# Spectra copied out of PSUM two banks at a time: a two-part layer on one core, with its stored order replaced

## The chip, the core and the metric

The program runs on one core of a Trainium2 chip. The time is device time in microseconds, the median of three runs. One core has five engines that run side by side: PE (TensorE, matmuls), DVE (VectorE), ACT (ScalarE), POOL (GpSimd) and SP, which here only issues DMAs. Matmul results land in PSUM, which has 8 banks of 512 fp32 columns per partition; ACT and DVE copy them from there to SBUF.

## The reference

Two independent halves are computed and put side by side in the output (2048 tokens, 640 + 640 columns). Part A is a gated long convolution, part B an attention with a compressive memory.

```
A: k_shift = 4-tap causal filter of k;  kv = k_shift * v
   y = irfft(rfft(kv, 2S) * rfft(ssm_k, 2S))[:S] + kv * ssm_D;   a = q * y
B: q, k, v = x @ wq, x @ wk, x @ wv          (32 heads of 20, segments of 512 tokens)
   for s in 4 segments:
       a_dot = softmax(q_s k_s^T * scale + mask) v_s
       a_mem = phi(q_s) M / (phi(q_s) z + 1e-6)
       o_s   = sigmoid(beta) * a_mem + (1 - sigmoid(beta)) * a_dot
       M, z += phi(k_s)^T v_s, sum phi(k_s)
   b = concat(o_s) @ wo
out = concat(a, b)                            (all inputs bf16)
```

## The kernel before

The whole program is recorded first and issued afterwards. `Layer` walks through the work and a `Recorder` notes each operation with its engine, its predecessors and its group of PSUM banks. `ORDER` is a stored permutation of the recorded operations, `BASE` gives each PSUM group its first bank, and `EVICT` has one digit per copy out of PSUM: "0" puts it on ACT, "1" on DVE. `Recorder.issue` then emits the operations in that order, so that on each engine, and on SP's queue of DMAs, the instructions stand exactly as the stored order has them. Every instruction carries line 257 in the profile, the line that issues it; the groups are told apart by the names of the tiles.

Part A runs in five passes `conv(dp)` of 128 channels. The filter (`kT`) and the filtered `kv` (`vt`) each go through `spectrum`: for each of 4 residues c, PE multiplies with the table `Wf` and makes two halves i = 0, 1 (real and imaginary part) of 512 columns, four matmuls of 256 columns each. They are copied to the tile `F`, which exists once. DVE then joins the residues in butterflies (`Xh` or `Kh`), multiplies the spectra (`product`, tiles `pq` and `Y`), and forms the inverse's inputs (`YB`, tile `Y`). `inverse` has for each c one PE group of 8 matmuls with `Wi` and one DVE multiplication with the loaded `q` (`pq<-ps,pq`), after which SP stores the rows. In the last pass each c is stored by itself, in 2 stores, 8 in all.

Part B has 8 units u, a segment and half of the heads each. `project(u)` makes `KQ` and `Va` (groups of five matmuls, 320 columns), turns `KQ` into `KQT`, and adds a row of bounds (`bT`, sent into `KQT` by small DMAs). `attend(u)` makes 10 score blocks of four banks; each is turned into the tile `ET` by two ACT exponentials of 1,024 columns. PE then multiplies `ET` with `Va` (and `PqT` with the memory `Mbd`), DVE divides. `project_out(s)` multiplies with `wo` and copies to `outb` (in the last segment: groups "ot" copied to `xT`, then five groups W copied to `PP`), and SP stores it. There are 80 score blocks and so 160 exponentials.

The copies of the spectra are made in this loop (lines 517 to 535); `FW` is the number of banks of a group:

```
for i in range(2):
    if i % FW == 0:
        g = self.group(FW, "F")
    ... four matmuls into g.ap[:, i % FW, :]
    if i % FW == FW - 1:
        self.evict(F[:, c, i - FW + 1:i + 1], g.ap, g)
```

Of the kernel before, what the change touches and what calls it, by code (L numbers as in the profile page):

```python
# [902 lines left out]
ORDER = r"""
c-jrtgMttW5Czb=Gk0=rwrjI(+um&3wry{=YqM?Jwr#$5zT(7@ToOeRNn%MN5hbZ4lPr>40wsl{lz1YNTk=SD$sqv}OQK3NNhPTztGFbTq?%14X>5rvd8M9E3J4^+#E_hlPx4D_O{Z}*nMRWOl3r738c8bw8eJ1=
PEDlgB)#O&1d>rQOAO7Txiqfi)~woCnoC2;qp7u^6p{>5TuMk&i7X|hl*E+6QbejsQK>G~q>+@CGNMve%1IN+Bqrshg5=eFT1;w4eyuE3q@q-kP!d<;X>!e=1vF4IYGO^Iku{2@(FPJE*|dc;liHG9(`rj;D>1dE
#L`+)P`gWeX(x51m2{O3Qb$@#AuX((rK5zFFp^1oYa0nGour3!llc-~i)sR0C`ELEjMgsFQ+i1s&8&TOj8@jD+D~t4RqZX|q>n6<eiBWqXkRI-#dU%%mvY))2FemyDigJome&-zNCru1T`Yqor54jNT1{(cbsZo>
WQY#cNjgXe>qs4?6||DBkd-o72kJ1Hq9wGX&d{M!QKxECt)oFYU7KlLt*14$zBbpHT1#u|8d)pDrGc)KS-M`f%MNL%vvs7j)AqVqw#Xa_*8Vy`8!4=bj*!OsPsgj+9POZ^WUl_y(egn*s@iuQp}%y4jFGVtBCU0t
Y?U_JR>#XUohzU8v;NR|I$uLsXj>)WWuB~-Vfsxb$pqOZV|Akp*KxW)Tj(Y^E(^7lMzUqPQzF_#31eYxvHp<d`dy~WE@`R1WQiV?JrZEMrK5Jz8M0SS$YJTKOSPN+mPOiGyXa5pu06D;9+M-oPd000+oHWRf=!jP
vQ_uXG&w2f<g}cZ5d9;kB#NDp12S2nn%gFwBGGN59+V3*Q)bB_S*?mS8p8}<^sru(n6_5G>QN=k9P6~69nnj2MZW1@`Kudrz1FwOLi;R&-?~Eo$!v*b!SY8}>Qz~#U9F9^wP@DOfY^3T4(Jy-s1YQN9nxL8TlZ*O
yCK_jyYA4PdQ6Y&UfrkB5d+tyxt-7mXkqazz9q8677?ATi|yBhc1F+YO*yCS?3Ub?a2DR~NEjrrrdAavwY}Yyut;J_EfktrWPFuyxG$$PH15fBIjxZpfbcl47xbcD(kQsBSM;j(vIlZaJ6K0cZPzuerLjlyLK@f&  # L910
ZD<drku|mymda9EZ)<6-?6EwP))p1f@Kl~icS~l;?WMezR}yGFETi?Y*OJ*{;*BInCTn7SEsLG7SjcLD$Y$9shvl?5NQ@*HXX7m?ZfP>4v-I{sGT2*rC$aI+`dMi!V`VKa(jm7!vg*iVc`cvCLwY>cCz{LhTYpP|
lt_itC}0UO&<0r|q(NGgv+`CA4>djt+FR>nkF=*%unc%+gYApGvl_^VAUwC>_SI^kgng8fcHf5BP#b3VG!yEgl#Q_ani&u5kBziKR>bb;T`g=`@Y`zRg}t<__$2jF2Su&8)k95uvj(`W-|fAPvJaLGf2|=Jp_o0;
7y42s*d%+Z*)h>x>l>|T9nlGuY=8;>Sq-afRV>JAS}kjhHpqdh)*iL3nt>hA60Pvrs++MXnqjg{u>`1N)%nI6u?ESUm}<YQHXE}s>aYpw+Gq>5TyQ?M3arRE_R+#}n$5KtHr;Zg2}7|dLo*D^@vW9;9^}PL`(*EQ
p3S#>m~9Jemc6oP`r5|Wb6sQMxX^ysI(uwmZIP|D#TK4FZKG|n&9>B**>YQ9`LV<*;fWQ1vN>9yE!Lwl+F`wgSY58PdfZ?e@Lmg|DywmoZMPj(1%*%;kr{!-P#mkRD0bOyi^3w<V|#6<ZLzIZ2K#KkMddb&#%An{
vgm?{JZOjPupP0Zwi(fRz=GJE$E+2*p%RZ<OIGF<)MR}&U~Kk9KMcex?TQd=L|hI+36w+(_D38Ba1+WQ5?eDCV{!o6vJHo$3b!I26R<pzFe&3R8M|W}dLTIiITXW?f+MgSdoUP7(2gD08-36VBQXjIxg9&O6T6U@
iI|<Ek&~rR8XcL1IXDj4I0l`VlG}NK7kQ6a`Is4*iY=I$wb+np_=MfqnPZWbnRuW3(S@0L0O@$0UD=&CI056)gSq&Wd6=Hhc$L?9jy;iqubG>tk(cLr29uDV1z3=USeQk4hwb@_MR}JetpY0Il=Wn9p0+p4$3eWp
Av|O6I1y*<oaOR9e9zk)%nNqW_F^B3F}L^U0A8{W{K&}|$WJWJ670oCEXgUjYzJ`&rC6F%F@mEwl4Upzec6vUIUTq7oG&<(!#RvcQQk{<Nq@=n_L*OJ3>7?w=k(DW!?B!!nYhHuoQ11amRD>Z=kqJSv7i_71-xb_
5scXw$5R;337p7DEat_1A*=c#KHx(x<{HdJexHN4oXiC{jCq)kg*bvGJdUX>;M2H_CoqN6IfF}C#b@%4-L<or#bD0iGAzduoX0uL<x+g-Z2qJ8T3ojq2ES#ut*n>xAH0BdSk9GP#noKHYJL%GxsEG%3D<E0Wqdtv
qlRC>9o)n%{Nz<!!v<c4x;Z_B8@Y*_`4D$;4_mmEk5JUN@iCs@H-r2S@8ba$;V;8@O|RuoQOd)4ZFev2ixJjW;2B;Zlt0HWuEa}(_BbBb^LTiV;1NBaNAkQL&l7oK-@%=%<4L@-NA+kP;L$yX*Y(IA#p`)}kLj-v
-}f_?-?M~%fU*4zZdw9Q>btm`2bs(ReHD`XA+AO$Z{V--77aaxr}i|S)>C>q&*163xwrIpXyJQU(JT30?qgg3fcBozGkIpu;!QlOzehXI?#=udvw2fL!lV3%R^G-7`*F_o)?UOvql0(!`M$tE;R_D4kyrQAJj1UT  # L920
=$(9?clN=4lBd|kyZSdY_Cemwhx-Wc?!Ej6dU#Lo?Z45-`}%i`^^qP*`}t4&MSuT;@jk$RVVsB7e;DFJ{r|>jI34C;bd)c2Xm}M}<Pmj(kM@a9o#c~!icj;^KHbOo44>(<e5x<@**?eD`*IKVrM|>B`3hg=D}9x(
@wL9e!)l1H^Nk)sUC;6aH~SXf=39N2Z}%O((|7wG-|PPY2lCQ8
"""
# [76 lines left out]
```

## Time and profile before

| what | value |
|---|---|
| median of 3 runs | 271.14 us (271.02 to 271.79) |
| profiled execution | 271.58 us, of it span 269.8 us |
| PE, DVE, ACT busy | 258.8, 249.6, 247.7 us |
| spectra copied on ACT | 71 of 512 columns, mean 682 ns of one |
| spectra copied on DVE | 9 of 512 columns, mean 683 ns of one |
| exponentials | 160 of 1,024 columns, mean 1,119 ns of one |
| granted TensorE clock | 1.00 |

The span goes from the first to the last instruction; the rest of the execution lies around it. Busy time counts an engine's instructions once where they overlap. The mean of one instruction includes its way through the engine's pipeline, which overlaps with the instruction behind it, so that the means of a full engine add up to more than its time. What one more instruction costs on a full engine is read from the starts of instructions that follow each other.

### The profile page before, as it was taken

What the parts mean: (1) busy time and instruction counts of PE and PEld (TensorE: products, weight loads), DVE (VectorE), ACT (ScalarE), POOL (GpSimd) and SP (SyncE); (2) the same over time, 40 slices, a digit from 0 to 9 for tenths busy, and PEclk for the clock granted to TensorE, in tenths of its full rate; (3) what the DMA queues carried; (4) which work ended last, traced back from release to release, by engine and by line L of the source; (5) the groups of instructions that cost most, each with busy time, mean ns of one, the idle gap of its engine ahead of it and who ended that gap; (6) DMA issues with size and microseconds to landing.
All of it is one profiled execution on the core that took longest, in us unless ns stands there. A gap on an engine that the chain in (4) does not pass through costs nothing.

```text
span 269.8 us, 10110 instructions
## 1 busy us (share of the span) xinstructions
PE 258.8 (96%) x4387; PEld 194.2 (72%) x4387; DVE 249.6 (93%) x400; ACT 247.7 (92%) x378; POOL 2.6 (1%) x9
## 2 busy tenths in 40 slices
PE   6999999999999999999999999999999999987994
PEld 3698677769777768767866778677776776655882
DVE  2899999999999999999999999999999999999960
ACT  1468899999999999999999999999999999999944
POOL 3000000000000000000000000000000000000000
PEclk9999999999999999999999999999999999999999
DMA  7998399995999799976999959987785289346043
GB/s 193 215 296 199 79 190 192 280 209 127 192 191 187 147 226 229 194 171 137 151 158 231 246 119 189 183 112 122 155 172 156 22 120 185 68 71 138 4 91 134
DMA packets 126716, 43.73 MB, mean 162 GB/s; under 512 B 117083, under 2 KB 124256, under 8 KB 126544
## 3 DMA queue, kind: packets, MB, share of 16 engines
q1 hardware_dynamic: 126512, 42.91, 80.7%
q8 instruction: 34, 0.56, 0.9%
q0 software_dynamic: 160, 0.19, 0.3%
q14 instruction: 10, 0.08, 0.1%
HBM read 14.11 MB, written 7.34 MB: 80 GB/s over the span
## 4 chain that ended last, share of the span: by engine, by line
PE 55%; ACT 35%; DMA 4%; issue 3%; DVE 1%; SPq 0%; ACTq 0%; DVEq 0%
PE ps L257 55%; ACT ET L257 23%; ACT F L257 5%; ACT PP L257 2%; ACT Va L257 2%; ACT KQ L257 2%; DMA out_dram<-outb 2%; DMA KQT<-KQ 1%; DMA pq<-in_A_q_dram 1%; ACT outb L257 1%; ACT xT L257 1%; ACT bT L257 0%; DVE xT L257 0%; DVE o_s L257 0%; DVE PP L257 0%
## 5 line engine op out<-in xcount | busy, mean ns | idle before, releaser
L257 ACT ACTIVATE ET<-ps 128x1024 bf16<-128x1024 f32 x160 | 163.6, 1119 | 1.1 <-PE ps L257 1.1
L257 PEld LDWEIGHTS <-xT 128*128 128x128 bf16 x640 | 58.1, 98 | 26.5 <-issue 4.8
L257 PE MATMUL ps<-wqkv,xT 128*128 128x320 bf16 x480 | 75.4, 299 | 0.4 <-DVE xT L257 0.2
L257 ACT CAST F<-ps 128x512 bf16<-128x512 f32 x71 | 41.9, 682 | 2.0 <-PE ps L257 2.0
L257 PE MATMUL ps<-Va,ET 128*128 128x21 bf16 x1280 | 40.1, 172 | 0.1
L257 PEld LDWEIGHTS <-ET 128*128 128x128 bf16 x1280 | 38.1, 96 | 1.9 <-issue 1.2
L257 PE MATMUL ps<-KQT 32*128 32x128 bf16 (+2 forms) x896 | 33.8, 238 | 0.8 <-ACT xT L257 0.4
L257 PEld LDWEIGHTS <-Wf 128*128 128x128 bf16 x320 | 29.2, 98 | 5.9 <-issue 1.7
L257 ACT CAST KQ<-ps 128x320 bf16<-128x320 f32 x55 | 25.8, 511 | 1.3 <-PE ps L257 1.1
L257 PE MATMUL ps<-wo,xT 128*128 128x320 bf16 (+4 forms) x160 | 25.7, 299 | 0.8 <-ACT ET L257 0.8
L257 PEld LDWEIGHTS <-KQT 32*128 32x128 bf16 x896 | 15.9, 91 | 11.7 <-issue 10.8
L257 PE MATMUL ps<-vt,Wf 128*128 128x256 bf16 x160 | 21.8, 272 | 0.1
L257 PE MATMUL ps<-kT,Wf 128*128 128x256 bf16 x160 | 21.8, 273 | 0.0
L257 PE MATMUL ps<-Y,Wi 128*128 128x256 bf16 x160 | 20.3, 273 | 0.6 <-ACT ET L257 0.3
L257 PE MATMUL ps<-Mbd,PqT 128*128 128x84 bf16 x96 | 18.1, 202 | 0.9 <-ACT ET L257 0.9
L257 DVE TENSOR_TENSOR Y<-Y,pq 128x2048 bf16<-128x2048 bf16 (+1 forms) x20 | 18.8, 946 | 0.1
L257 DVE TENSOR_TENSOR pq<-Xh,Kh 128x2048 bf16<-128x2048 bf16 x15 | 18.2, 1215 | 0.1
L257 PEld LDWEIGHTS <-Wi 128*128 128x128 bf16 x160 | 14.9, 98 | 4.2 <-issue 2.2
L257 ACT ACTIVATE PP<-KQ 128x1280 bf16<-128x1280 bf16 x12 | 16.4, 1368 | 0.0
L257 PEld LDWEIGHTS <-kr 128*128 128x128 bf16 x116 | 14.8, 148 | 1.7 <-issue 0.2
L257 ACT CAST Va<-ps 128x320 bf16<-128x320 f32 x29 | 14.7, 549 | 0.9 <-PE ps L257 0.9
L257 PE MATMUL ps<-pack 32*128 32x128 bf16 x512 | 13.8, 215 | 1.1 <-ACT ET L257 0.9
(90 smaller groups left out, 365.4 us busy)
## 6 DMA issues: line engine op xcount, KB each, us to landing
vt<-in_A_v_dram SPq DMA_DIRECT2D x10, 256.0 KB
pq<-in_A_q_dram SPq DMA_DIRECT2D x10, 256.0 KB
turned<-kT SPq DMA_DIRECT2D x4, 512.0 KB
kT<-turned SPq DMA_DIRECT2D x4, 512.0 KB
out_dram<-pq SPq DMA_DIRECT2D x8, 256.0 KB
out_dram<-outb SPq DMA_DIRECT2D x12, 160.0 KB
kb<-kr SPq DMA_DIRECT2D x6, 256.0 KB
Wf<-c_wf SPq DMA_DIRECT2D x4, 256.0 KB
```

The costliest lines, as they stand in the source:

```text
L257: f(*[fix(a) for a in args], **{k: fix(v) for k, v in kw.items()})
```

## The change

`FW` goes from 1 to 2. The two halves of a residue then share one group of two neighbouring banks, and one copy of 1,024 columns takes both after the second half's matmuls. There are 40 copies of spectra in place of 80, 38 on ACT and 2 on DVE. No matmul and no DMA is added or removed. Since the recorded operations are others, `ORDER`, `BASE` and `EVICT` are new as a whole: all engines and SP's queue have another order, and some other copies change between ACT and DVE.

```
--- before.py
+++ after.py
-EVICT = ("0101000110000010100000101000...
+EVICT = ("0000100010000001000000000000...
...
-KQW, FW, WW = 1, 1, 1
+KQW, FW, WW = 1, 2, 1
...
 ORDER = r"""
-c-jrtgMttW5Czb=Gk0=rwrjI(+um&3wry{=YqM?Jwr#$5zT(7@ToOeRNn%MN5hb...
+c-jrtgLW7S5Cy=ydw1KEscqY~o!Yi-+fHiRwr$(CZNK*ub0#lxAvPi+4iX{}vLg...
...
 BASE = r"""
-c-l>q0hYxe2m>Pu-v7p{L+ao9+FFH>1e?0o)Ht^kT4%O+7pwOjM5Oka@AEazxDo...
+c-l>q3lfAd2t$EVdjA_Qgn+B#*p}ZTqDoyZM@()$M_%qC*P6G(Qg%sO<XyYSwWP...
```

By kind, the copies of the two programs stand on the engines as follows; the copies of `PP` and `taps` are all on ACT in both.

| tile, columns | ACT before | DVE before | ACT now | DVE now |
|---|---|---|---|---|
| F, 512 | 71 | 9 | 0 | 0 |
| F, 1,024 | 0 | 0 | 38 | 2 |
| KQ, 320 | 55 | 9 | 52 | 12 |
| Va, 320 | 29 | 3 | 30 | 2 |
| bT, 512 | 8 | 0 | 7 | 1 |
| KQT, 512 | 7 | 1 | 7 | 1 |
| kT, 512 | 2 | 2 | 3 | 1 |
| xT, 512 | 4 | 1 | 5 | 0 |
| xT, 640 | 2 | 2 | 3 | 1 |
| outb, 320 | 19 | 5 | 19 | 5 |

The first place is ACT's list ahead of the first exponential (`ET`), from the copies that stand behind the filter's spectrum on, before:

```order
L257 CAST KQ<-ps 128x16x20 x3
L257 CAST KQT_87<-ps 128x4x128
L257 CAST KQ<-ps 128x16x20
L257 CAST KQT_87<-ps 128x4x128 x3
L257 CAST F_101<-ps 128x512 x3
L257 CAST bT_109<-ps 128x512
L257 CAST F_101<-ps 128x512 x3
L257 CAST Va_85<-ps 128x16x20
L257 CAST KQ<-ps 128x16x20
L257 CAST Va_85<-ps 128x16x20
L257 CAST KQ<-ps 128x16x20 x2
L257 ACTIVATE ET_114<-ps 128x1024
```

And now, with the filter's spectrum (the four wide copies):

```order
L257 CAST kT_100<-ps 128x4x128 x3
L257 CAST KQT_87<-ps 128x4x128 x4
L257 CAST F_101<-ps 128x1024 x4
L257 CAST KQT_87<-ps 128x4x128
L257 CAST bT_109<-ps 128x512
L257 CAST Va_85<-ps 128x16x20 x2
L257 CAST F_101<-ps 128x1024 x3
L257 CAST KQ<-ps 128x16x20 x2
L257 ACTIVATE ET_114<-ps 128x1024 x2
```

The 512-column copies have become wide ones, the first unit's copies of `KQ` and `KQT` that stood between the two spectra have moved ahead of them, and of the second unit's `KQ` two copies, not three, stand ahead of the first exponential; on PE as well one group of that projection has moved from ahead of the first score block to behind it.

The second place is the end of DVE's list, from the last butterflies of the fifth pass (`Y<-Xh`) on, before:

```order
L257 TENSOR_TENSOR Y_98<-Xh_104 128x2x512
L257 TENSOR_TENSOR pq_79<-ps,pq_79 128x4x128 x4
L257 CAST xT_97<-ps 128x512
L257 RECIPROCAL rr_118<-ps 128x32
L257 TENSOR_TENSOR o_s_110<-ps,rr_118 128x4x80 x2
L257 RECIPROCAL rr_119<-ps 128x32
L257 TENSOR_TENSOR o_s_110<-ps,rr_119 128x4x80 x2
```

And now:

```order
L257 TENSOR_TENSOR Y_98<-Xh_104 128x2x512 x2
L257 TENSOR_TENSOR pq_79<-ps,pq_79 128x4x128 x3
L257 RECIPROCAL rr_118<-ps 128x32
L257 TENSOR_TENSOR o_s_110<-ps,rr_118 128x4x80
L257 TENSOR_TENSOR pq_79<-ps,pq_79 128x4x128
L257 TENSOR_TENSOR o_s_110<-ps,rr_118 128x4x80
L257 RECIPROCAL rr_119<-ps 128x32
L257 TENSOR_TENSOR o_s_110<-ps,rr_119 128x4x80 x2
```

The fourth multiplication with `q` has moved behind the division of the last but one head group. On PE this goes with the inverse's groups: before, all four of the fifth pass stood ahead of the last score block (segment 3, second half, head group 3); now two of them stand behind it.

The third place is the start of SP's queue, before:

```order
L257 DMA Y_98<-in_B_x_dram 128x640 x2
L257 DMA ident<-c_ident 128x128
L257 DMA Y_98<-in_B_x_dram 128x640
L257 DMA wqkv<-in_B_wk_dram 128x5x320
L257 DMA Y_98<-in_B_x_dram 128x640
L257 DMA_TRANSPOSE kr<-in_A_k_dram 128x2048
L257 DMA Wf<-c_wf 128x1024
L257 DMA kT_99<-in_A_ssm_k_dram 128x2048
```

And now:

```order
L257 DMA Y_98<-in_B_x_dram 128x640 x4
L257 DMA ident<-c_ident 128x128
L257 DMA wqkv<-in_B_wk_dram 128x5x320
L257 DMA wqkv<-in_B_wq_dram 128x5x320
L257 DMA kT_99<-in_A_ssm_k_dram 128x2048
L257 DMA_TRANSPOSE kr<-in_A_k_dram 128x2048
L257 DMA Wf<-c_wf 128x1024 x3
```

All four loads of x now stand ahead of the identity, and the weights of q and the filter ahead of the transposing load of k.

More of the change, by code (lines that the diff above doesn't have):

```diff
@@ L897 @@
 TAP2 = (2, 3, 4)
-EVICT = ("0101000110000010100000101000000000000000000000000000000000000000001100000000001000000011010000100100000000000000000000000000000000000000"
-         "000010000100000000000100000000000000000000110000000010010010101001000100000000010000100100010000000")
-KQW, FW, WW = 1, 1, 1
+EVICT = ("0000100010000001000000000000000000000000000000100010000000011000100100000000000000000001100000000000000000000000000000010000000000000000"
+         "00000001010100000101000010000010000110000010111000000000000")
+KQW, FW, WW = 1, 2, 1
 KSW = (1, 1, 1, 1, 1)
@@ L903 @@
 ORDER = r"""
-c-jrtgMttW5Czb=Gk0=rwrjI(+um&3wry{=YqM?Jwr#$5zT(7@ToOeRNn%MN5hbZ4lPr>40wsl{lz1YNTk=SD$sqv}OQK3NNhPTztGFbTq?%14X>5rvd8M9E3J4^+#E_hlPx4D_O{Z}*nMRWOl3r738c8bw8eJ1=
-PEDlgB)#O&1d>rQOAO7Txiqfi)~woCnoC2;qp7u^6p{>5TuMk&i7X|hl*E+6QbejsQK>G~q>+@CGNMve%1IN+Bqrshg5=eFT1;w4eyuE3q@q-kP!d<;X>!e=1vF4IYGO^Iku{2@(FPJE*|dc;liHG9(`rj;D>1dE
-#L`+)P`gWeX(x51m2{O3Qb$@#AuX((rK5zFFp^1oYa0nGour3!llc-~i)sR0C`ELEjMgsFQ+i1s&8&TOj8@jD+D~t4RqZX|q>n6<eiBWqXkRI-#dU%%mvY))2FemyDigJome&-zNCru1T`Yqor54jNT1{(cbsZo>
@@ L907 @@
[L907 to L922, printed above, removed]
+c-jrtgLW7S5Cy=ydw1KEscqY~o!Yi-+fHiRwr$(CZNK*ub0#lxAvPi+4iX{}vLg%P0&pZo5+p@rBtr}&M+&4wDx^jZ<U|65LILDM8l*)n5Q+#e#6*77Mik^mJfuT<2=X94vLXXwAu8U>Pl*Q85As#A;i>!**RUE+
@@ new lines @@
+zX?<{Gom9CLTN@klZg6TiX*gsl;`qCiXyxQ>L*bxhJq-J7xGq0pb(1SyF}8+8b#~lois#L4MGI{A=H>!9u-g)Wl#={Q4!I!0V*L7kx&w)PzRM!8qqa|)<qM%me6=3jSx#?YdwTT6;wx61ZXvUme#0=F#1JWqA3E<
+49(F3VbBWg&;~Wo7VXgi9nl4y&>3CPP#bAwt)g)?wWif+h@;cdO4I0H`6sQlh0Z`cZK;Vgu{PEw+6_I?9aXiOCefGjN+u(zCe!&?fLhvIlWT2Fr|Gp9>S$e^iCIXY9W;Zc)C8JPXQK!5X)5iF{8~WgAfs;7teQ>Z
+Yj(|~nRN;pXcp~*9GX*$YkTdBTsjvew4KgFN$rP@+D7}MpcdAq+Dxl!O>L`%w37}*J*}@bbP1N?hAu;A9e|5^QwO1lUecm^UyJDpJ*f-vKo_Bl4#qPq$6|EV6<CSY7=o!-h4Xq>*WiM7(;nJg?`cmRfnJ(h`|B{|
+(NmgNPwO=uj_X=Zhhi-TXpolIC%O*LH5_(eCw5^yN@-~=qh)miD(EOw)RE||FVII{p|5VkR&2*cY{GNg(Q{f!cViFs;w7HyW<1mV*oOlcs}m877dlSI;|(U@r5?n19i?M*EXHAo7UyUks)td6qcH}<bhggXe)?M9
@@ new lines @@
+;{!fot`67N_=FMqMn~#fyu(8ssE_eT58*Se>K9zr!TMMWaF8CsExn=zd0XG=44tX(^cW`SB%Q2BF;PPhtRXrH@Aae3(^)!2r|JUzpeHb2b21mpuq=;bntswH`dPo?B&O>rY{6-q!C5TRrTPuuaYoN-Q5Iu(EY#ol
+gGKrSKe1e&V1?$DFZxwi>MC8V-}Nbe;V)L}8a<D-DkRtGdR6`dM5M56(2^|0e9X_kdJaGI0t)e;{!;L#7Umx<$K3p_LA;1px=AnL3N9lLv-2u)FrQTBZr!6sXIO?~cwR#UMr3)0Vg**^H@%J<$S*2|WC8CYG{bP4
+26DT)Q0^gs5ha2I%5B_1C7RsCErgcDOv1<vB~cia(O5ttF|34>Doo1gj3(6>RU%0YMwajrUAAa-)?_k9k*%77rKA>1%Y78#10-hxCSnY!&3)X@qb$v1%**YJ#e}TL9V{ZTC5+TzY@T5p)@MOE%et(`b8Nu4Y{>I`
+h*+|dF{OlT)<%4Uc&xzyY0O=W&t^Q%%Zwv&rKB`xOrBsdX~9<9p+)5Y53(hTOIax+<)k%JG8NnM3R5!;D@hy1m#eHOm1U>y(zJ{x>6n4nn4TG#iJ6&&UD%CHd7W9=g!^>A9?%=?%62@cx7eN?c$#VL2(#I3X18><
@@ new lines @@
+n+aqOJF*iyv#K28VOEi9a))=BP}18yCX$oPVE36=hVm4%F^LT0a88i!?7^Pw#nBwgz3k0P?8664CQ0Q2lgk*6;7C4X3cJXZ){p%;fR8wkgV>j&IFW-ni76$Rxn!?Sl$)H)DNG?#IgKIAYxyi##&JBeSTdWyAW3fJ
+We9UyTFGj;rGh->Oit%4&Solk$~nwqY2+n~+H20>T&A+rmQLpJ6{pA(=C{<6UY>EX<dF=LQ3}|5eq;{IXd#l*Cdmg@mrPdJYRMbE<8#)Ow|v2)dQ9s}4XGmyq>wd~#?nZdNNt%eGbEE_mQVb`*)pF+Y@&T;F)L_I
+rJ2l;7E(`IN-oPH&84`dv9D|;S>+o`+Dw@xrR)cP@;iU=HzU{|MzqqFP5v^_!dhzyXW?yyWtTD*+E!Xw+hzfl*<fO7hm;n^O4vUJSvf0j+bxo{5wi-m#iH15Yb$PBZN0UVg^X+)EUN9X=vG$_>oRLE9ps2cv%R*@
+mfInVVKFV1g|gVzNh(?#i)*!Ps!WsGwwO62r*xEfR>!K_T3aSHt%e=8<GNf{$U3WROSpnZY$@l;N>;ME)>-DsGS;*D7T*$BLQ7<ec+9#;Vw*2X?6|G5gSN_6+bTA&)!b#9t*bP&ZqmpW$O)@rNqsq!`9fJNi)4wc
@@ new lines @@
+;aFKJ-Q}c>lT+5%dP)yTY8$PYHMbVl)LPmmYhvB4hqbbJ9@7U&YwKyTyqBG}_}<&ravgg~A4}ltdB!%exAc*|wt)%#tVQ&5cHTC#p9OkyZ)07ozoqc5HbAy;EBi}ZYiI4PgY}h;cFnq3Rl8x=t&{Dy1J+LlN;Ml`
+E2Xmyv<nu=2ip)EYDev&ZR2>kWW#KgME2n}!fx6iyKN(7l&z7`cFRUd8Xse0ZMBTF%XZbqS#*!#>*R`!x52Ve()uRZEL&xW+_AeB%~Sh5TPs^+x9pN6p3Zm3Hi_%oWsgMhoif3qdP+~__w9jY@C}mDGkIpu<~wYs
+W%1$i&_38l+bgmCkv+C27HlIV#6H=6d1_fbj%W8Ap4)T!K6z%}?7RK21M<RV+H*T3LuHtZk@YgmKHFFOVh81=y|UN##{Sq_dvEXTh$QlVme~K=Py21~|I6jS{>QtUcXxC5P@c<+`E(mChoywiu;O083wme|@Gu_M
+3;9vW>$5GNhx70r!SnkuS!_$Juov-?UfNGcDL*b#?4+EQjht$eY_b*gnqJEn+9Eq8XC%Fs@v>gdgS@;~@Y<fo>w5#Q=ncJ+SN1Ai)z3;bZ|cpxhR?I=KF#La96KlHrJ2|9y57U<c`v^z7o@k(wM%kWdiq6a<c+<F
@@ L923 @@
+xA2zU$}h_mxhD7Ip*)h--p1ScO}Qm)y}ftvj^4>f_z>^oeZ8}H^)BAe$M{%(BK>`&UzZ#5SZ>Q5c_8;?l#ljtKHi7=03YbXe7Fzt!9Kw!da#H1Qd?kCe6mmSss0~tS+>s
 """
 BASE = r"""
-c-l>q0hYxe2m>Pu-v7p{L+ao9+FFH>1e?0o)Ht^kT4%O+7pwOjM5Oka@AEazxDoSwZQ?ptXT33&bJp3Po?V<|MMU1*1(wd<y%%fo&^Grv&xFYx34Riju$qsTK-rI1Qc=W?GfSg&ZK3(H3fE3}Pit?kt#%O6_!Blo
-?oV5xK`1J!3BCfccn91P_Xf-tJ831Yy3i`SkgyA@zxkhwWwyfqMo;^*(H3^SYbK-hrt3G~z_spPT2c39gV`Ml_>>v_ybvd$Bg%@~`NZk8`ed)`e4Un`3Dbd+q`KU@FrvVj_9yM0{^{O6AM$xDG)y=(`_GNxj&*PP
-3<Zw1r$y{$f7|V84&9aU7$-TyUmxG{A28mjSk7MlE98i>tMMGtKdv&T&$(&z?+pF{kIx1i
+c-l>q3lfAd2t$EVdjA_Qgn+B#*p}ZTqDoyZM@()$M_%qC*P6G(Qg%sO<XyYSwWP;^ef9yLI<w62a{qEwJ40+&Y5%flW(daBy5p*9AYK_S$SbtpTos|>OhFXnEv5^ahgiYsVF!Un@D@fG&YG&d?)IVBbv}c&{e~zu
@@ L928 @@
+UcojR39Gf93L0A-4Lm_TTG4~dO2+mYy`37$YIl}3(7&M0Fwb>Zt5z4P$?{D`Xa38+AE^5s(E5TsU{xyH*@L`74U8Pd{tY#QR$mSJ3py=59hbgC_)VPe1URb+X#0EhWI1Q8X&<v6X11kpcK2x-WSZ*z7YH)Wls<N<
+JK;0&@u%VU#SiB>P<tvW*?wyq1(^
 """
```

## The prediction

> **What bounds the kernel now.** I read the windows first, cut where the work changes its limit: from the start to the first score block on PE (32.28), from there to PE's first product with the last but one pair of exponentials (257.31), and the rest. The columns are the stretch, its length, then busy time and instructions of each engine.
>
> ```profile
> core 0: us, PE busy (x) PEld busy (x) DVE busy (x) ACT busy (x) POOL busy (x), PEclk, DMA share, GB/s
> 0.00:32.28 32.28, 29.87 (x258) 22.12 (x260) 24.53 (x48) 19.26 (x39) 2.57 (x9) 1.00 0.80 198
> 32.28:257.31 225.03, 220.08 (x3986) 165.43 (x3986) 221.90 (x346) 223.06 (x332) 0.00 (x0) 1.00 0.85 160
> 257.31:269.80 12.49, 8.82 (x147) 6.60 (x144) 3.18 (x7) 5.36 (x9) 0.00 (x0) 1.00 0.38 112
> ```
>
> In the first stretch PE is the fullest (29.87 of 32.28); ACT has little to do before there are scores. In the long middle ACT (223.06 of 225.03) and DVE (221.90) are both full, 99% each. PE's 220.08 is modelled, since matmuls overlap. In the last 12.5 us only PE is left, until its end at 266.14. The chain that ended last says the same of the end:
>
> ```profile
> 249.42 0.94 ACT ET L257
> 250.35 0.04 issue
> 250.40 15.75 PE ps L257 x300
> ```
>
> So a microsecond counts on PE before 32.28 and after some 250 to 257, and in between only if it is taken from ACT and DVE both. The waits then tell how much a smoother order could give back (engine and tile, whom it waited for, total, times, longest):
>
> ```profile
> ACT ET L257 <- PE ps L257: 1.1, 4, 0.4
> PE ps L257 <- ACT ET L257: 3.4, 10, 0.5
> ```
>
> No wait is long. What is lost lies in many small gaps, which the price list below makes visible.
>
> **What a copy costs.** Start, length, engine, instruction, count; a group's length holds the overlap of its members, so I take start to start.
>
> ```profile
> 61.62 1.40 ACT L257 ACTIVATE PP<-KQ 128x1280 bf16<-128x1280 bf16 x1
> 62.78 0.56 ACT L257 CAST KQ<-ps 128x320 bf16<-128x320 f32 x1
> 63.08 1.18 ACT L257 ACTIVATE ET<-ps 128x1024 bf16<-128x1024 f32 x1
> 64.00 1.72 ACT L257 CAST F<-ps 128x512 bf16<-128x512 f32 x3
> 65.42 1.47 ACT L257 ACTIVATE PP<-KQ 128x1280 bf16<-128x1280 bf16 x1
> 66.72 1.99 ACT L257 ACTIVATE ET<-ps 128x1024 bf16<-128x1024 f32 x2
> 68.55 1.63 ACT L257 CAST F<-ps 128x512 bf16<-128x512 f32 x3
> 69.96 2.06 ACT L257 ACTIVATE ET<-ps 128x1024 bf16<-128x1024 f32 x2
> ```
>
> Two exponentials take 68.55 - 66.72 = 1.83, so 0.915 each (0.92 at 63.08); three copies of 512 take 1.41 (and 1.42), so 0.47 each; a copy of 320 takes 0.30 to 0.31; an exponential of 1,280 takes 62.78 - 61.62 = 1.16. No ACT copy of 1,024 columns is in the trace. Its nearest row is ET, with the same columns, source and output: 0.91. The other end is two copies of 512, 0.94. A wide copy then saves 0.03 of a pair, between 0 and 0.05. 36 such pairs stood on ACT: about 1 us in all, not more.
>
> The Trainium skill, "ScalarE: Activation LUTs", section What ACT_TABLE_LOAD costs, gives an activation with immediate scale and bias as 186 ns + 0.833 ns a column, of which back-to-back ones overlap by about 93 ns. By that two copies of 512 would cost 1.04 us and a wide one 0.95, a saving of 0.09; the rows have 0.94 and 0.91, and so ACT's list would fall some 2 us further than in the sum below.
>
> **ACT's list in the middle.** Its rows for the stretch from 32.28 to 257.31 (busy time, mean of one, idle before):
>
> ```profile
> L257 ACT ACTIVATE ET<-ps 128x1024 bf16<-128x1024 f32 x159 | 162.7, 1120 | 1.1 <-PE ps L257 1.1
> L257 ACT CAST F<-ps 128x512 bf16<-128x512 f32 x59 | 35.4, 699 | 0.3 <-PE ps L257 0.2
> L257 ACT CAST KQ<-ps 128x320 bf16<-128x320 f32 x48 | 22.8, 523 | 0.1
> L257 ACT ACTIVATE PP<-KQ 128x1280 bf16<-128x1280 bf16 x11 | 15.1, 1376 | 0.0
> L257 ACT CAST Va<-ps 128x320 bf16<-128x320 f32 x27 | 13.8, 557 | 0.0
> L257 ACT CAST outb<-ps 128x320 bf16<-128x320 f32 x19 | 9.5, 502 | 0.5 <-DMA out_dram<-outb 0.5
> L257 ACT CAST bT<-ps 128x512 bf16<-128x512 f32 x7 | 4.6, 651 | 0.0
> ```
>
> 158 of the 159 exponentials count (the last belongs to the last score block), 47 of the KQ copies, and two copies of xT are not shown. At the prices: 158 x 0.91 = 143.8, 59 x 0.47 = 27.7, 93 copies of 320 x 0.31 = 28.8, 9 of 512 x 0.47 = 4.2, 11 x 1.16 = 12.8; sum 217.3. The stretch took 225.0, so 7.7 us were lost between ACT's instructions. In the new order the same stretch of ACT's list, counted, has 158 ET, 31 wide copies (28.2), 93 of 320, 6 bT and 1 xT (3.3), 11 PP: 216.9. That is 0.4 less (between 0.2 and 0.8, as the copy's price is rounded).
>
> **DVE's list in the middle.** From the first score block to the last butterfly of the fifth pass, on which PE's last inverse products wait:
>
> ```profile
> L257 DVE CAST F<-ps 128x512 bf16<-128x512 f32 x9 | 6.1, 683 | 0.1
> L257 DVE CAST KQ<-ps 128x320 bf16<-128x320 f32 x9 | 4.3, 485 | 0.6 <-ACT xT L257 0.6
> L257 DVE TENSOR_TENSOR o<-ps,rr 128x640 bf16<-128x640 f32 x16 | 13.0, 815 | 0.2
> L257 DVE TENSOR_TENSOR Xh<-Xh 128x1024 bf16<-128x1024 bf16 x20 | 13.6, 684 | 0.0
> 254.25 1.28 DVE L257 TENSOR_TENSOR pq<-ps,pq 128x512 bf16<-128x512 f32 x2
> ```
>
> From 320 to 640 columns out of PSUM the mean grows by 330 ns, so a wide DVE copy, which the trace does not have, is 815 + 384 x 1.03 = about 1.21 (bounds: 0.82 of the 640 columns and 1.37 of two copies). Five copies of 512 leave this stretch (-3.4), one wide one comes (+1.2), a KQ copy comes and a Va copy goes (0), one bT comes (+0.7), and three butterflies of 0.68 now stand ahead of the first score block (-2.1): -3.6. Six instructions fewer also means six overlaps fewer, 0.08 each (two multiplications of 0.685 take 1.28), so -3.1.
>
> **The end.** PE's inverse groups, and SP's stores:
>
> ```profile
> 252.23 1.91 PE L257 MATMUL ps<-Y,Wi 128*128 128x256 bf16 x16
> 254.07 0.41 PE L257 MATMUL ps<-pack 32*128 32x128 bf16 x16
> 254.63 1.92 PE L257 MATMUL ps<-Y,Wi 128*128 128x256 bf16 x16
> 254.97 6.70 SPq L257 DMA_DIRECT2D out_dram<-pq  x8
> 261.76 1.03 SPq L257 DMA_DIRECT2D out_dram<-outb  x2
> 264.88 2.23 SPq L257 DMA_DIRECT2D out_dram<-PP  x4
> 266.17 0.58 ACT L257 CAST PP<-ps 128x512 bf16<-128x512 f32 x1 [0.34 <-PE ps L257]
> ```
>
> Two groups take 254.07 - 252.23 = 1.8 us. Two of them now stand behind the last score block, so the path over ACT grows: 225.0 to 257.31, then 8.8 of PE to 266.14, becomes 225.0 - 0.4 and 8.8 + 1.8, which is +1.4 if every lost microsecond stays lost. The path over DVE was 222.1 (to 254.34) and 11.5 of PE from 254.63; it loses 3.1, and 1.6 of PE's rest, since only 9.9 follow the third inverse group (8.8 + 1.8 - 0.7 of products ahead of it): -4.7. Before, both ended together; now DVE has slack, and ACT alone is full.
>
> How much of ACT's 7.7 comes back with that? At least nothing. At most 5.0, if ACT then loses no more than DVE did (its busy 219.32 of the 222.06 to its last butterfly, 2.7):
>
> ```profile
> 32.28:254.34 222.06, 217.11 (x3942) 163.14 (x3945) 219.32 (x343) 220.73 (x329) 0.00 (x0) 1.00 0.86 161
> ```
>
> I take the middle, 2.6, since no row is nearer to either end. The first stretch has one projection group of five matmuls fewer ahead of the first score block:
>
> ```profile
> 30.82 1.52 PE L257 MATMUL ps<-wqkv,xT 128*128 128x320 bf16 x10
> 32.28 0.40 PE L257 MATMUL ps<-KQT 32*128 32x384 bf16 x8
> ```
>
> Ten take 1.46, five 0.7. But all four loads of x are queued ahead of the identity and more loads ahead of that of k, so I count half, -0.35 (between -0.7 and +0.7). The first of the eight stores waits for the third inverse group, 7.9 us ahead of PE's end, not 11.2 as now (254.97 against 266.14); with 6.7 for the eight and 1.0 for the two behind, the four last stores start 0.2 before PE's end, not 1.3. They need 2.0 to the last issue, which so comes 0.7 later; half of it counts, +0.35 (0 to +0.7).
>
> **The sum.** -0.4 + 1.8 - 2.6 - 0.35 + 0.35 = -1.2. The profiled execution took 271.58 (span 269.8), the median is 271.14; the change is taken off the median: 269.9. 0.3%, 0.8 us, is about what a measurement of this kernel can tell from no change.
>
> **Rivals.** *Nothing to measure.* ACT's list is as long as before, and a part of the lost time just covers the +1.4: 0.6 to 2.2 of the 7.7 return. For it speaks that ACT's waits in the rows are few; against it, that DVE, the other full engine, gets slack. Time 271.1.
>
> *The end gets longer, slower.* The two inverse products and eight stores behind the last score block cost 1.8, and nothing comes back, because ACT's gaps were its own and DVE's slack is useless. It decides once less than 0.6 of ACT's lost time returns. Time 272.5.
>
> *Banks.* A wide copy starts only after the second half's matmuls, 0.44 later (four of 0.11), and holds both banks until its end: 2 x (0.9 + 0.9) in place of 2 x (0.44 + 0.47), twice as long. If that doubles PE's 3.4 us of waits for ET's copies, and ACT starves for as long, 273.3 stands. Against it: 40 x 1.8 us are 4% of eight banks over the middle. The Trainium skill, "Perfetto Trace Analysis", section Matmuls, wants independent matmul groups to rotate through banks, so that the evacuation of one overlaps the next group's matmuls. That rule speaks against the wide copy, and names this rival; the trace of before cannot decide it.
>
> *A real saving per copy.* If the means of the rows were the price, a pair would fall from 2 x 0.699 to 1.12 and 31 of them save 8.6, 262.5. The means of the middle's rows add up to more than its length, so no; a third of it, 268, is possible if many gaps go with the instructions.
>
> **How the numbers follow.** Forecast 0.42, nothing to measure 0.28, longer end 0.17, banks 0.06, saving per copy 0.07. Of the forecast 0.02 falls within 0.3%, and of the middle case 0.01 on either side counts as faster or slower: faster 0.48, same 0.28, slower 0.24. The range takes the ends of the return, 5.0 (-3.6) and 0 (+1.4): 267.5 to 272.5. It leaves out most of the banks and the far saving, and so under 2 in 10. The forecast's own range is 268.0 to 270.3.
>
> **What would show it.** ACT's wide copies should start 0.91 apart from the next; the busy share of DVE in the middle should fall by a point or more while ACT stays at 99%; the first score block should stand at 31.6 to 32.3, PE's end 9 to 11 us behind the last score block, and the last stores close behind one another. Wrong would be the forecast if ACT's share falls too, if waits of PE for ET or F grow past 5 us, or if the last store is issued over 2 us after PE's end.

## The result, and the profile after

The changed kernel takes 273.23 us (median of 5 runs, 272.67 to 273.75), the kernel before beside it 271.02 (270.49 to 271.79): 1.0078 times as long, 95% interval 1.0053 to 1.0103. It is 0.8% slower, 2.2 us, where 1.2 us less was forecast. The profiled execution took 272.75 with a span of 271.0, against 271.58 and 269.8 before, so the two profiles differ by 1.2, not by 2.2: the one before lies 0.56 over its median, the one after 0.48 under its own. Differences of stages below are of these two profiles; what an edit costs is taken from the timed runs. Of the 107 executions of the changed kernel and of those made from it below, 15 show a granted TensorE clock of 0.984 to 0.994 in place of 0.996 or more and took 0.6 to 3.1 us longer than the median of the others of their kernel; none of 132 of the kernel before is under 0.997, so a few tenths of a median below can come from there.

The windows, cut at the same two events as in the prediction (first score block on PE, PE's first product with the last but one pair of exponentials):

```profile
0.00:30.96 30.96, 28.52 (x253) 21.63 (x255) 20.79 (x43) 19.80 (x33) 2.62 (x9) 1.00 0.83 211
30.96:256.47 225.51, 219.81 (x3975) 165.79 (x3975) 221.92 (x342) 223.58 (x304) 0.00 (x0) 1.00 0.86 158
256.47:271.00 14.53, 10.56 (x160) 8.19 (x160) 4.78 (x10) 5.75 (x9) 0.00 (x0) 0.95 0.37 105
```

The first stretch is 1.3 shorter (30.96, was 32.28), the middle 0.5 longer (225.51, was 225.03), the rest 2.0 longer (14.53, was 12.49). DVE's column matters most: in the first stretch it did 43 instructions and 20.79 us, where it did 48 and 24.53 before, and in the middle it is as full as before (221.92, was 221.90). The slack on which the forecast stood is not there: DVE is busy for 98.4% of the middle, 98.6% before. (The clock of 0.95 in the last row falls behind PE's end: until 267.1 it is 1.00.)

The waits (engine and tile, whom it waited for, total, times, longest):

```profile
PE ps L257 <- ACT ET L257: 3.6, 10, 0.5
ACT F L257 <- PE ps L257: 2.6, 3, 1.4
ACT ET L257 <- PE ps L257: 0.7, 3, 0.3
```

Before, PE's wait for ET stood at 3.4 and ACT's for ET at 1.1; ACT's for the spectra's matmuls, 2.6, are three waits in all, and all three end ahead of the first exponential. None of these waits tells where the time went.

The wide copy on ACT's timeline, start to start:

```profile
64.52 3.98 ACT L257 CAST F<-ps 128x1024 bf16<-128x1024 f32 x4
68.38 1.04 ACT L257 ACTIVATE ET<-ps 128x1024 bf16<-128x1024 f32 x1
87.68 1.04 ACT L257 CAST F<-ps 128x1024 bf16<-128x1024 f32 x1
88.57 0.48 ACT L257 CAST Va<-ps 128x320 bf16<-128x320 f32 x1
```

One copy is followed 0.89 later; four in a row took 3.86, 0.97 each. Over the copies on ACT that are followed without a gap the median is 0.90.

ACT's list in the middle (busy time, mean of one, idle before):

```profile
L257 ACT ACTIVATE ET<-ps 128x1024 bf16<-128x1024 f32 x158 | 161.0, 1133 | 1.0 <-PE ps L257 0.7
L257 ACT CAST F<-ps 128x1024 bf16<-128x1024 f32 x31 | 33.0, 1135 | 0.1
L257 ACT CAST KQ<-ps 128x320 bf16<-128x320 f32 x48 | 23.7, 535 | 0.2 <-PE ps L257 0.2
L257 ACT ACTIVATE PP<-KQ 128x1280 bf16<-128x1280 bf16 x11 | 15.2, 1390 | 0.0
L257 ACT CAST Va<-ps 128x320 bf16<-128x320 f32 x28 | 15.2, 560 | 0.0
L257 ACT CAST outb<-ps 128x320 bf16<-128x320 f32 x19 | 10.1, 556 | 0.6 <-DMA out_dram<-outb 0.6
L257 ACT CAST bT<-ps 128x512 bf16<-128x512 f32 x6 | 4.1, 686 | 0.0
L257 ACT CAST xT<-ps 128x512 bf16<-128x512 f32 x3 | 1.7, 625 | 0.0
```

Three lines at the stretch's two ends bear on the count:

```profile
30.82 0.76 ACT L257 CAST KQ<-ps 128x320 bf16<-128x320 f32 x2
255.30 1.12 ACT L257 CAST xT<-ps 128x512 bf16<-128x512 f32 x2
256.49 1.94 ACT L257 ACTIVATE ET<-ps 128x1024 bf16<-128x1024 f32 x2
```

One of the 48 copies of KQ starts at 30.82, ahead of the stretch, and is left out, as the prediction left one out before. At the prediction's prices, with 0.90 for the wide copy: 158 x 0.91 = 143.8, 31 x 0.90 = 27.9, 94 copies of 320 x 0.31 = 29.1, 9 of 512 x 0.47 = 4.2, 11 x 1.16 = 12.8; sum 217.8 of 225.5. So 7.7 were lost between the instructions, as before.

The end, on PE, DVE and SP, and in the chain that ended last:

```profile
254.22 1.91 PE L257 MATMUL ps<-Y,Wi 128*128 128x256 bf16 x16
255.09 1.28 DVE L257 TENSOR_TENSOR Y<-Xh 128x1024 bf16<-128x1024 bf16 x2
256.06 0.40 PE L257 MATMUL ps<-KQT 32*128 32x384 bf16 x8
257.19 1.03 PE L257 MATMUL ps<-Y,Wi 128*128 128x256 bf16 x8
258.51 1.03 PE L257 MATMUL ps<-Y,Wi 128*128 128x256 bf16 x8
258.98 6.19 SPq L257 DMA_DIRECT2D out_dram<-pq  x8
265.27 1.03 SPq L257 DMA_DIRECT2D out_dram<-outb  x2
266.39 1.88 SPq L257 DMA_DIRECT2D out_dram<-PP  x4
```

```profile
249.38 7.08 PE ps L257 x157
256.47 10.57 PE ps L257 x160
```

DVE's last butterflies end at 256.37, after the last score block has started; before they ended at 254.34 (253.66 + 0.68), 2.1 ahead of it. Two inverse groups follow behind the block, and PE needs 10.57 from the last but one pair of exponentials to its end (8.83 before).

### The profile page after: what moved, and what is told of

The parts are those of the page before. It is cut to its first block, busy times and chain, and to the rows that moved or that the text cites. A ratio compares the mean times of both kernels' runs of the same rounds, so it can differ in the third digit from the quotient of the medians.

```text
span 271.0 us, 10072 instructions
## 1 busy us (share of the span) xinstructions
PE 258.9 (96%) x4387; PEld 195.6 (72%) x4387; DVE 247.5 (91%) x393; ACT 249.1 (92%) x345; POOL 2.6 (1%) x9
## 5 line engine op out<-in xcount | busy, mean ns | idle before, releaser
L257 ACT CAST F<-ps 128x1024 bf16<-128x1024 f32 x38 | 39.8, 1113 | 2.7 <-PE ps L257 2.6
L257 PEld LDWEIGHTS <-Wf 128*128 128x128 bf16 x320 | 30.0, 98 | 5.2 <-issue 1.3
L257 PE MATMUL ps<-vt,Wf 128*128 128x256 bf16 x160 | 20.4, 273 | 0.1
L257 PE MATMUL ps<-kT,Wf 128*128 128x256 bf16 x160 | 19.8, 272 | 0.0
L257 ACT CAST Va<-ps 128x320 bf16<-128x320 f32 x30 | 16.1, 551 | 0.3 <-PE ps L257 0.3
L257 PE MATMUL ps<-pack 32*128 32x128 bf16 x512 | 14.4, 216 | 1.8 <-ACT outb L257 0.8
```

The costliest lines, as they stand in the source:

```text
L257: f(*[fix(a) for a in args], **{k: fix(v) for k, v in kw.items()})
```

## The experiments

All ratios are against the kernel before, timed beside each, with their 95% intervals; the changed kernel stands at 1.0078.

**1. The new order without the widening (split).** In the function that makes a spectrum:

```
-self.evict(F[:, c, i - FW + 1:i + 1], g.ap, g)
...
+for h in range(2):
+    self.evicts = e
+    self.evict(F[:, c, h], g.ap[:, h], g)
```

> The changed kernel with its stored order, its banks and its engines, but each of the 40 wide copies of the spectra written as two copies of 512 columns, one behind the other on the same engine. It undoes the widening and keeps the new order. In the profile after, a wide copy on ACT is followed 0.90 later by the next instruction, one of 512 0.48 later, so ACT's list grows by 38 x 0.05 = 1.9. Theory 'order' (the loss lies in the new order: two inverse groups behind the last score block, and a first stretch in which DVE loses 10.5 us, 7.6 before): the time does not fall; 0 to +1.9 over the changed kernel. Theory 'banks' (the wide copy itself holds PE and ACT up): the loss goes with it, back to the kernel before, -1.5 to -2.2 against the changed kernel.

273.32, ratio 1.0073 (1.0050 to 1.0096): as slow as the changed kernel, with an interval of some 0.6 us on either side of both. So the width of the instruction is not the loss, and its 1.9 us on ACT are not a gain that shows; the loss sits in what came with it, the order. Two things of the pair stay as they were: its banks are still neighbours, which run 11 takes up, and the first half's copy still stands behind the second half's matmuls, which no run takes up.

**2. The old order with the widening (wide_old, and later wide_old2).** The pairs' copies are merged in the order before, its copies of 1,024 on ACT 36 times and on DVE 4 times.

> The kernel before in its own stored order, with only the spectra's copies widened: the matmuls of a pair's earlier half stand directly ahead of those of the later half, 36 wide copies on ACT and 4 on DVE in place of 71 and 9, and the PSUM banks dealt out anew to fit pairs of neighbours. By the prices ACT's list falls by 71 x 0.477 - 36 x 0.903 = 1.4 and DVE's by 9 x 0.60 - 4 x 1.22 = 0.5. Theory 'order': no loss, 0 to -1.4 against the kernel before, as the widening is worth a little by itself (a disturbed order may take some of it: up to +0.5). Theory 'banks': slower than before by 1 to 2.2, the change's whole loss.

304.45, ratio 1.1232 (1.1198 to 1.1266): 33 us slower, far off either expectation. The waits of this kernel:

```profile
ACT F L257 <- PE ps L257: 15.4, 18, 1.7
ACT ET L257 <- PE ps L257: 12.7, 26, 1.1
PE ps L257 <- ACT F L257: 12.4, 16, 1.1
PE ps L257 <- ACT ET L257: 8.1, 20, 0.7
```

ACT waits 28 us for PE, and PE 20 us for ACT. The halves of a pair stood up to 110 places apart in the order of the kernel before, and a pair needs two neighbouring banks at once.

> The kernel before in its own order with the copies widened, as in wide_old, but the later half of each pair drawn ahead to the earlier one, and the banks dealt out by when they come free in time and no longer by their place in the order. Same copies and engines as wide_old, which took 304.5. Theory 'banks': most of the 33 us goes, 275 to 285. Theory 'the widened copies in that order': it stays above 295.

284.5, ratio 1.0499 (1.0477 to 1.0522). With pairs drawn ahead and banks dealt by the time at which they come free, 20 of the 33 us are gone (two executions). Put into the old order in either of these ways, the widening costs far more than the change did; whether a better dealing would fit it in was not tried. Both the merging's direction and the banks were changed between the two runs, so their shares are not told apart.

**3. DVE relieved, in both kernels (dve_less, old_dve_less).**

```
-V.tensor_tensor(out=F[:, 2:4], in0=F[:, 0:2], in1=F[:, 2:4], op=ALU.subtract)
+V.tensor_tensor(out=F[:, 2:3], in0=F[:, 0:1], in1=F[:, 2:3], op=ALU.subtract)
```

> The changed kernel, with DVE's second butterfly of each spectrum (2,048 columns, 1.13 us, 10 of them) done on half of its columns: 0.53 less each, 5.3 us less on DVE in all, nothing else changed. The left out half leaves the spectra wrong. Theory 'DVE is still full' (the new order's first stretch used up the 3 us that its list is shorter, so ACT's lost time could not come back): the time falls by 1 to 2.6, as the prediction had it for a DVE with slack. Theory 'ACT's gaps are its own': no change, within 0.5.

271.84, ratio 1.0039 (1.0020 to 1.0057): 1.1 to 1.4 faster than the changed kernel. (Of two such numbers, here and below, one is the difference of the ratios and the other that of the medians.) From the first to the last score block, of the changed kernel and of this run:

```profile
30.96:256.06 225.10, 219.41 (x3968) 165.59 (x3968) 221.51 (x341) 223.22 (x304) 0.00 (x0) 1.00 0.86 159
31.34:255.50 224.16, 219.07 (x3968) 165.49 (x3968) 217.43 (x340) 222.93 (x304) 0.00 (x0) 1.00 0.87 159
```

DVE has 4.1 us less to do in this stretch, and the stretch is 0.9 shorter.

> The kernel before, with the second butterfly of each spectrum on half of its columns, as in the run of the changed kernel with DVE relieved: 5.3 us less on DVE in all. The left out half leaves the spectra wrong. It tests the prediction's largest term in the kernel it was read from: that DVE's slack of 3.1 gives back 2.6 (0 to 5.0) of ACT's lost time. By that term it should fall by 2.6 or more. Theory 'a quarter' (the same elasticity as in the changed kernel, 1.4 for 5.3): -1.0 to -1.8. Theory 'ACT alone': 0, within 0.5.

271.05, ratio 0.9994 (0.9976 to 1.0012): nothing. This run is the test of the prediction's largest term in the kernel that it was read from, and the term fails. The windows from the first to the last score block, of the kernel before and of this run:

```profile
32.28:256.48 224.20, 219.25 (x3970) 164.81 (x3969) 221.21 (x345) 222.48 (x331) 0.00 (x0) 1.00 0.85 160
31.47:255.23 223.76, 218.68 (x3971) 164.53 (x3971) 217.16 (x344) 222.36 (x331) 0.00 (x0) 1.00 0.84 160
```

DVE's busy time falls by 4.0, the stretch by 0.4 and ACT's busy time not at all: what DVE saves it now waits.

**4. ACT relieved, in both (act_less, old_act_less).**

```
-self.evict(F[:, c, i - FW + 1:i + 1], g.ap, g)
+n = 1 if dp and c == 0 else 2
+self.evict(F[:, c, 0:n], g.ap[:, 0:n], g)
```

In the kernel before, each of the two copies of such a block takes 256 of its 512 columns.

> The changed kernel, with the wide copies of the first row block in passes 1 to 4 (8 copies) taking 512 columns in place of 1,024: 8 x 0.43 = 3.4 us less on ACT (one of them is DVE's in no pass but the last, so 3.0 to 3.4), nothing else changed. The other half of those blocks keeps old values. Theory 'ACT's gaps are its own' (ACT alone bounds the middle): the time falls by 2.5 to 3.4. Theory 'DVE is still full' (both bound it): it falls by less than half of that, 0 to 1.5.

> The kernel before, with the spectra's copies of the first row block in passes 1 to 4 (16 copies of 512) taking 256 columns: 16 x 0.21 = 3.4 us less on ACT (one or two of them are DVE's: 3.0 to 3.4). The other half of those blocks keeps old values. Beside the same cut in the changed kernel, where 3.0 to 3.4 us less on ACT gave 2.1. If ACT bounds both kernels alike: -1.8 to -2.4. If the order before has ACT and DVE end together and neither helps alone, as the prediction read it: 0 to -1.

In the changed kernel 271.11, ratio 0.9999 (0.9984 to 1.0014), 2.1 less; in the kernel before 270.02, ratio 0.9953 (0.9933 to 0.9973), 0.9 to 1.3 less. ACT counts in both, some twice as much in the new order, and in neither for the whole cut.

**5. PE relieved, in both (pe_less, old_pe_less).** The second of the two accumulated matmuls is left out:

```
+if kind == "K" and dp and c % 2 == 0 and h:
+    continue
...
```

> The changed kernel with 32 of the spectra's matmuls left out (the second of two accumulated ones, in the filter's spectra of passes 1 to 4, every other row block): 32 x 0.11 = 3.5 us less on PE, spread over the middle. It leaves those spectra wrong. In the middle PE's list is 206 of 225, and relief of ACT by 3.0 to 3.4 gave 2.1, of DVE by 5.3 gave 1.4. Theory 'ACT and DVE bound it, PE has slack': 0 to -0.5. Theory 'PE's part in the loop of banks counts' (a copy waits for its matmuls, and these for a bank): -1 to -2.5.

> The kernel before with the same 32 matmuls left out, 3.5 us less on PE. There, relief of DVE by 5.3 gave 0.0 and of ACT by 3.0 to 3.4 gave 1.0, so the larger part of its bound is elsewhere. Theory 'PE's part in the loop counts': -1 to -2.5, more than ACT's relief gave. Theory 'ACT and DVE bound it, PE has slack': 0 to -0.5.

271.67, ratio 1.0017 (1.0001 to 1.0034), 1.6 less than the changed kernel; 270.70, ratio 0.9977 (0.9960 to 0.9994), 0.4 to 0.6 less than the kernel before. The order before gives little for relief of DVE, ACT or PE (0, 1 and 0.5), the new one something for each (1.1, 2.1, 1.6). Each of these has an interval of 0.5 to 0.8 us, so for one engine alone the two orders are hardly told apart; that all three differ the same way is what speaks for it.

**6. The end moved into the old order (old_tail).** PE's order there, one row a group:

```
-inverse group 3, inverse group 4, last score block, products 1 to 4
+last score block, products 1 to 3, inverse group 4, product 4, inverse group 3
```

> The kernel before, with two of the last pass's four inverse groups (the third and fourth on PE) and their two DVE multiplications moved behind the last score block, to where the changed kernel has them: one behind the third product of the block's next pair, the other behind the fourth; their stores follow. Two PSUM banks of those groups chosen anew. Theory 'tail' (the new order's end costs what the prediction gave it, two groups of 0.9 on PE alone): +1.4 to +1.8 against the kernel before. Theory 'hidden' (PE's work there only changes places, the loss of the changed kernel is in its middle): 0, within 0.5.

272.13, ratio 1.0040 (1.0021 to 1.0060): 1.1 slower, between the two expectations. In its trace PE waits 1.11 for an exponential ahead of the last score block, with no inverse group to fill the gap, and the two groups follow behind:

```profile
255.15 0.40 PE L257 MATMUL ps<-KQT 32*128 32x384 bf16 x8 [1.11 <-ACT ET L257]
256.98 1.03 PE L257 MATMUL ps<-Y,Wi 128*128 128x256 bf16 x8
258.29 1.03 PE L257 MATMUL ps<-Y,Wi 128*128 128x256 bf16 x8
```

In the old order the end alone costs half of what the change cost. That this is its price in the new order too isn't shown: there the first two inverse groups (254.22) stand directly ahead of the last score block, and its line (256.06) shows no such wait.

**7. The old end in the new order (new_tail).** From the fourth last score block on, the order of the kernel before.

> The changed kernel with the end of its order, from the fourth last score block on, replaced by that of the kernel before: all four inverse groups stand ahead of the last score block. The choice of engine for the copies in that end is that of the kernel before too, and its banks are dealt anew; everything ahead of it as in the changed kernel. Theory 'tail': faster than the changed kernel by 1.0 to 1.8. Theory 'DVE is late' (in the new order DVE reaches its last butterflies too late, 256.3, so the inverse groups can't stand earlier without PE waiting for them): no change against the changed kernel, within 0.6, and PE waits for DVE ahead of the last score block.

272.54, ratio 1.0063 (1.0040 to 1.0085): 0.4 to 0.7 less than the changed kernel, which the intervals hardly separate. From the first to the last score block:

```profile
30.90:257.30 226.40, 220.85 (x3975) 166.64 (x3975) 223.25 (x344) 223.21 (x303) 0.00 (x0) 1.00 0.85 158
```

With the same end as the kernel before, and so with the same work ahead of the last score block, this stretch takes 226.40 where the old order takes 224.20. The 1.4 won ahead of the first score block is given back in it, and 0.8 more. It holds 1.6 more of PE's busy time and 2.0 more of DVE's than the old order's, which the shorter first stretch left behind. Where old_tail puts the end at half of the loss, this run puts it at a fifth to a third; the rest lies ahead of the last score block.

**8. Where DVE counts (dve_early, dve_late, dve_first).** All six butterflies of both spectra of one pass, on columns 0 to 255 of 512:

```
-V.tensor_tensor(out=T, in0=F[:, 0:2], in1=F[:, 2:4], op=ALU.add)
+r = slice(0, 256) if dp == 1 else slice(0, 512)
+V.tensor_tensor(out=T[:, :, :, r], in0=F[:, 0:2, :, r], in1=F[:, 2:4, :, r], op=ALU.add)
...
```

> The changed kernel with DVE relieved in one place only: the six butterflies of both spectra of the second pass (61 to 89 us in its trace) on half of their columns, 2 x (2 x 0.53 + 4 x 0.27) = 4.3 us less. The left out halves leave that pass wrong. 5.3 us less, spread over all passes, gave 1.4. Theory 'DVE is late from the first stretch on' (it is 3 us behind its list there, and carries that to the end): relief early is worth as much as relief spread, -0.8 to -1.4. Theory 'late' (DVE is on the path only where its last butterflies stand ahead of the inverse groups): relief early is lost again in DVE's waits, 0 within 0.5.

> The same cut, 4.3 us less on DVE, in the last pass (210 to 231 us in the trace of the changed kernel). Both theories expect a gain here, -0.8 to -1.4; by 'late' it is all of the gain that relief of DVE can bring, and up to -2; if relief is worth nothing here either, the 1.4 of the spread cut comes from between the two places.

> The changed kernel with the butterflies of the first pass (25 to 42 us) on half of their columns, 4.3 us less on DVE there; the left out halves are zeroed once by POOL early in the kernel. The same cut in the second and in the last pass gave 1.3 and 0.8. Theory 'first pass' (DVE's work there is on the path, as adding 3.5 to it in the old order cost 3.7, and the new order has it 1.1 later): faster by 2 or more, at or under the kernel before. Theory 'like any other' : -0.5 to -1.3, and the half of the loss that the end leaves open is not the first pass's DVE.

271.90, 272.48 and 272.35; ratios 1.0037 (1.0013 to 1.0060), 1.0042 (1.0019 to 1.0065) and 1.0038 (1.0026 to 1.0050). Second, last or first pass, 4.3 or 5.3 us: by the ratios DVE's relief is worth 1.0 to 1.1 in the new order, by the medians 0.8 to 1.4, and the intervals don't tell the places apart. A limited debt that can be paid anywhere ahead of the end would fit. The theory that the first pass's DVE makes the other half falls.

**9. Both relieved (new_tail_dve_less).** New_tail with the cut of dve_early.

> The changed kernel with the end of the kernel before and with the second pass's butterflies on half of their columns (4.3 us less on DVE). The changed end alone brought it 0.7 nearer, DVE's relief alone 1.1 to 1.3. If they add up, it stands within 0.5 of the kernel before (+0.0 to +0.5). If both are the same loss, seen from two sides, it stays at +0.9 to +1.4.

272.99, ratio 1.0073 (1.0051 to 1.0094): over both expectations, and no faster than new_tail. So with the old end no gain from DVE's relief shows in the new order. The six executions spread from 272.06 to 274.23, too far to tell nothing from a few tenths. It looks as if DVE's debt and the new end were one loss seen from two sides, but by what path is not shown. It is not that the two late inverse groups wait for DVE's last butterflies: in the changed kernel the third group starts at 257.19, 0.8 behind the butterflies' end at 256.37, and in dve_less the distance is the same (256.64 and 255.81). What DVE's relief gives is won ahead of the last score block (run 3). What is left, 1.6 to 2.0 by these two runs, is for the most part not DVE's.

**10. DVE made late in the old order (old_dve_more, old_tail_dve_more).**

```
-V.tensor_tensor(out=T, in0=F[:, 0:2], in1=F[:, 2:4], op=ALU.add)
+for n in range(2 if dp == 0 else 1):
+    V.tensor_tensor(out=T, in0=F[:, 0:2], in1=F[:, 2:4], op=ALU.add)
...
```

> The kernel before with DVE made late by itself: in the first pass two butterflies of each spectrum (1.13 and 0.60) are done twice, 3.5 us more on DVE between 22 and 42 us, with the same results. Theory 'DVE late from the first stretch' (it explains the half of the loss that the end leaves open): +0.5 to +1.2 against the kernel before. Theory 'slack' (in that order DVE has room, as 5.3 less gave 0.0): 0 within 0.4, and the open half lies in how the new order's middle is written.

> The kernel before with both: the two inverse groups behind the last score block, and DVE's 3.5 us more in the first pass. If the two are the changed kernel's loss and add up, +1.6 to +2.3 against the kernel before; if DVE's lateness is no part of it, +0.7 to +1.3, as the moved end alone.

274.74, ratio 1.0136 (1.0120 to 1.0152), and 276.14 (four executions), ratio 1.0192 (1.0176 to 1.0208). Both are over every expectation: 3.5 us more in the first pass cost 3.7, all of it. They show that load there is on the path in the old order; they do not show that it is in the new one, where relief at the same place (dve_first) gave only what relief elsewhere gave. The moved end adds 1.4 on top, about what it cost alone.

**11. Each half in a bank of its own (unpaired).** Order and engines of the changed kernel, 80 copies of 512, each with a bank of its own. The two copies stand one behind the other in the place of the wide one.

> The new order with 80 copies of 512 in the places of the 40 wide ones, and each half in a bank of its own, dealt out anew by when banks come free (26 of the 40 pairs no longer lie in neighbouring banks). The split run kept the pairs' banks and took 273.3. Theory 'neighbours' (a pair's need of two neighbouring banks costs the open 1.1 to 1.6): 271.5 to 272.3. Theory 'order' (the banks' form is worth nothing, the new order itself is slower ahead of the last score block): 273 to 274.

274.10, ratio 1.0138 (1.0093 to 1.0183): slower than split, if anything. That a pair needs neighbours is not what costs the open half; that holds for this dealing of the banks, the only one that was run. It leaves one part of the pair as it was: with copies and groups of four matmuls matched in their order, the first half's copy starts before the second half's matmuls end in 29 of the 40 pairs in the trace of the kernel before, in none in the changed kernel, and in 4 each in split and in unpaired. What these later copies cost, no run shows.

## Why the prediction was wrong, point by point

- **Copy and list.** The wide copy's price was right: 0.91 taken, 0.90 measured, 0.89 to 0.97. But ACT's list in the middle did not fall by 0.4; it rose from 217.3 to 217.8, by 0.5. I had counted the stored order from the first exponential to the 158th, and the stretch is cut by PE's time. A copy of KQ listed ahead of the first exponential ran behind the first score block (30.82), and the two of xT listed behind the 158th exponential ran ahead of the stretch's end (255.30): 94 copies of 320 columns and not 93, 9 of 512 and not 7. The widening's own saving of 0.05 a pair, 1.9 in all, is not in the time: split and the changed kernel differ by 0.1, with intervals of some 0.6 each.
- **DVE's list.** The -3.1 failed in the same way. The three butterflies "ahead of the first score block" are so only in the order; in time the block ran 1.3 earlier, the first stretch ended with 3.7 us less of DVE's work done than before, and two butterflies of 2,048 columns that stood ahead of it or across it before now stand behind it, so that the middle has as much busy time of DVE as it had. (Of the nine copies of 512 in the prediction's row for this stretch four lie ahead of it; its sum took the five.)
- **The return of ACT's lost time**, -2.6, is the step that decides. It had two premises. That DVE gets slack: it did not (221.92 of 225.51). That DVE's slack gives ACT its lost time back: in the kernel before, run 3 gave DVE 5.3 and got 0.0. ACT's loss was 7.7 and is 7.7: nothing came back. That ACT and DVE end together and are both 99% busy did not mean that they wait for each other. Without this term the sum is +1.4.
- **The end**, +1.8, is right in size by the trace (10.57 against 8.83); timed alone it is 1.1 in the old order, and undone in the new one 0.4 to 0.7.
- **Stores**, +0.35: the last store is issued 1.2 behind PE's end (268.27 against 267.04), 0.3 later than before. Right.
- **The first stretch**, -0.35, bounds -0.7 to +0.7: it was -1.3, outside. Yet it is no gain, since work that was not done there came behind it. Its error of 0.95 and the list's of 0.9 cancel in the sum; that is luck.
- Sum of the trace: -1.3 + 0.5 + 0.0 + 1.7 + 0.3 = +1.2, as the spans say.
- **The signs.** None of the three signs named for a wrong forecast came: ACT stayed at 99%, PE's waits for ET at 3.6, the last store at 1.2 behind PE's end. What gave it away were two signs named for a right one: DVE's share fell by 0.2 points and not by one or more, and the first score block stood at 30.96, ahead of 31.6.
- **The rivals.** "The end gets longer, slower" is what happened in kind: the two groups behind the last score block, nothing back from ACT and, in the kernel before, DVE's slack useless. It gave 272.5; the time is 0.7 over that and over the range. "Nothing to measure" is out by the result, "a real saving per copy" by run 1. "Banks" gave 273.3, and 273.2 is the time, but by luck: its mark, PE's waits for ET doubled, is out by the rows (3.4 and 3.6). Its other part, that a copy starts only behind the second half's matmuls, is in the trace (run 11), and no run gives its price. The Trainium skill's rule that independent matmul groups rotate through banks ("Perfetto Trace Analysis", section Matmuls) bears on run 2. There pairs put into an order not written for them cost 33 us, and 13 us with other banks and the pairs drawn ahead; no run tells the banks' part of it from the merging's.
- **Open.** Some 1.0 to 1.7 of the loss stand ahead of the last score block. Shown is what they are not: the wide instruction (run 1) and the pair's neighbouring banks as dealt in run 11; DVE's part of them is small at most (9, and dve_first). The new order reacts to relief of PE and ACT some two to three times as much as the old one, within the wide intervals of runs 4 and 5. That it keeps PE and ACT more tightly bound to each other would fit, and so would the later start of the first half's copies; no run here took either apart.
